# A fused decayed-attention, gated-MLP and max-MLP kernel: two chunks to one state rescale, row-wise gains, and a new order of steps

## The chip, the cores and the metric

The kernel runs on one core of a Trainium2 chip. The time is what the device reports for one execution of the whole program, in microseconds; a profiled execution has a span beside it, from the first to the last instruction. The engines named here are TensorE (PE: matrix products and transposes), VectorE (DVE), ScalarE (ACT), GpSimd (POOL) and SyncE (SP, which issues the transfers).

## The reference

Three stages follow each other. The first is a recurrence over 768 positions for 4 batches of 8 heads, with a state of 48 by 48 in a head; the decay of a position is complex and its magnitude is capped at 0.999.

```python
scale = np.minimum(mag, 0.999) / (mag + 1e-06)
a_re_n, a_im_n = (a_re * scale, a_im * scale)
for t in range(S):
    ar, ai = (a_re_n[:, :, t, :, None], a_im_n[:, :, t, :, None])
    new_re = ar * S_re - ai * S_im
    new_im = ar * S_im + ai * S_re
    kv = np.einsum('bhd,bhe->bhde', k[:, :, t], v[:, :, t])
    S_re, S_im = (new_re + kv, new_im)
    y[:, :, t] = np.einsum('bhd,bhde->bhe', q[:, :, t], S_re)
```

Its output, 3072 tokens of 384, goes through an MLP with a norm and a gate, and then through a product that keeps the largest of three.

```python
xn = x / rms * rms_g
silu = g * (1.0 / (1.0 + np.exp(-g)))          # g = xn @ w_gate
x = (silu * (xn @ w_val)) @ w_out              # 384 -> 1536 -> 384
h = np.maximum(np.maximum(x @ w1, x @ w2), x @ w3)
out = h @ w_out2                               # 384 -> 768 -> 384
```

The weights come as float64.

## The kernel before, in words

The positions are cut into six chunks of 128, and the batches into two pairs, which gives twelve units x0 to x11: unit n is the chunk n//2 of the pair n%2. A unit computes products of the decays inside a group of eight positions (the steps scan, VectorE), then across groups and up to the chunk's start (pre, many short steps on VectorE that write the tile G and the tile ET), spreads them (pa), multiplies them into q (qh) and their reciprocal into k (kr, kh), transposes both (tq, tk), and forms scores (qk), a mask (msk, GpSimd) and the output (pv). For the state that later chunks read it copies the scaled k into rows of positions by eight transfers on SP (kn1 and kn0, L801, tile kn), multiplies it with v on TensorE (kv0 and kv1, L912), and adds that to the state W (wa). As the decays are counted from the chunk's own start, the state is then rescaled by the decay of the whole chunk: a small product brings the decay into place (pw, L725, and t12, L730), two transfers swap the halves of W (wd, L929 and L930), and three steps on VectorE multiply and add (wu with x, y or z; they are recorded at the helper's line L341).

Two units give the 512 tokens of a block; blocks m0 to m5 run the MLP (g and v products at L1100 to L1102, then silu, gate, the split of the hidden values into two float16 parts uh and ul, and the products acc) and the max-MLP (h at the same lines, mx, hh, hl, and the output products om at L1254 to L1256). All weights and activations of the MLPs are float16 pairs, so each product is three. The blocks m0 and m1 are cut into two pieces of 256 tokens, each of which needs one unit alone. The steps big (L1243) keep a largest square for a range check at the end.

The float64 weights become float16 pairs in 60 conversions c0 to c59, each of 128 by 384: low (ScalarE, L421), join and sign (VectorE, L426 and L430), high (either of them), and for the lower half a difference, in 24 of the 60 as two products on TensorE (dif, L438 and L439) and otherwise on VectorE (rest). The first MLP's weights are multiplied by the gains rms_g, which gcl brings into the tile gsc (L382 and L383) and diag into the matrices down (L375). Transfers l0 to l59 read the weights once more, for a check of their range.

Every step has a name, and a table ORDER lists all the names in the order in which they are issued. Each engine takes its own instructions from that one list, strictly in order; a letter behind a name says which engine takes a step that could go to either. Semaphores, put in by the framework, make an instruction wait for its operands and for its buffer.

## Time and profile before

| what | value |
|---|---|
| three runs | 1017.63, 1018.71 and 1027.02 us; median 1018.71 us |
| profiled execution | 1017.69 us, its span 1016.0 us |
| TensorE busy | 941.9 us, 93% of the span |
| VectorE busy | 818.4 us, 81% |
| ScalarE busy | 462.5 us, 46% |
| GpSimd busy | 60.9 us, 6% |

A busy time is the union of the instructions' records and says nothing of who waits for whom. The page's strip of 40 slices shows where in the span an engine is busy, and at which share of full speed TensorE's clock was granted; the table by stretches gives the same for chosen stretches in microseconds; the timeline has the start, the duration and the idle time ahead of single instructions with what ended it.

### The profile page before, as it was taken

What the parts mean: (1) busy time and instruction counts of PE and PEld (TensorE: products, weight loads), DVE (VectorE), ACT (ScalarE), POOL (GpSimd) and SP (SyncE); (2) the same over time, 40 slices, a digit from 0 to 9 for tenths busy, and PEclk for the clock granted to TensorE, in tenths of its full rate; (3) what the DMA queues carried; (4) which work ended last, traced back from release to release, by engine and by line L of the source; (5) the groups of instructions that cost most, each with busy time, mean ns of one, the idle gap of its engine ahead of it and who ended that gap; (6) DMA issues with size and microseconds to landing.
All of it is one profiled execution on the core that took longest, in us unless ns stands there. A gap on an engine that the chain in (4) does not pass through costs nothing.

```text
span 1016.0 us, 16755 instructions
## 1 busy us (share of the span) xinstructions
PE 941.9 (93%) x6231; PEld 589.8 (58%) x6231; DVE 818.4 (81%) x1966; ACT 462.5 (46%) x877; POOL 60.9 (6%) x63
## 2 busy tenths in 40 slices
PE   1576998999999999999999999999999999999997
PEld 0254767855789886555556455556455565544443
DVE  4999999999899999649897488897459999875352
ACT  5666777665545573415563233643215352012110
POOL 1020010010010100000010001100000100000000
PEclk9677999999999999999999999999999999999999
DMA  6454565642231313023113023013012435872001
GB/s 170 125 144 133 129 174 147 187 130 57 66 74 44 65 53 69 16 54 67 34 47 76 1 59 86 9 47 75 1 44 70 118 109 174 260 235 62 1 1 35
DMA packets 84651, 87.50 MB, mean 86 GB/s; under 512 B 51920, under 2 KB 69200, under 8 KB 84560
## 3 DMA queue, kind: packets, MB, share of 16 engines
q1 hardware_dynamic: 84288, 85.95, 31.1%
q8 instruction: 51, 0.84, 0.3%
q10 hardware_dynamic: 272, 0.39, 0.2%
q14 instruction: 40, 0.33, 0.1%
HBM read 70.78 MB, written 4.72 MB: 74 GB/s over the span
## 4 chain that ended last, share of the span: by engine, by line
PE 71%; DVE 7%; ACT 1%; issue 1%; POOL 1%; DVEq 0%; ACTq 0%
PE gv L1100 7%; PE gv L1101 7%; PE gv L1102 7%; PE hm L1100 7%; PE hm L1101 7%; PE hm L1102 7%; PE yp L866 3%; PE acc L1100 3%; PE acc L1102 3%; PE acc L1101 3%; PE tp L810 3%; PE qk L834 3%; PE om L1254 2%; PE om L1256 2%; PE om L1255 2%; PE kp L912 2%
## 5 line engine op out<-in xcount | busy, mean ns | idle before, releaser
L849 POOL TENSOR_SCALAR_AFFINE_SELECT P<-P 128x512 f32<-128x512 f32 x48 | 57.4, 1205 | 780.1 <-ACT P L330 543.7
L1100 PE MATMUL gv<-XH,wvh 128*128 128x256 f16 (+1 forms) x288 | 94.4, 328 | 4.4 <-ACT sg L1128 4.4
L1102 PE MATMUL acc<-uh,wol 128*128 128x256 f16 (+1 forms) x288 | 93.9, 326 | 2.2 <-DVE wol L267 2.0
L1101 PE MATMUL gv<-XL,wgh 128*128 128x256 f16 (+1 forms) x288 | 94.3, 327 | 0.8 <-DVE XL L264 0.8
L1100 PE MATMUL gv<-XH,wgh 128*128 128x256 f16 (+1 forms) x288 | 94.3, 327 | 0.7 <-ACT XH L330 0.7
L1102 PE MATMUL gv<-XH,wvl 128*128 128x256 f16 (+1 forms) x288 | 94.4, 328 | 0.1
L1100 PE MATMUL acc<-uh,woh 128*128 128x256 f16 (+1 forms) x288 | 93.9, 326 | 0.6 <-ACT uh L330 0.2
L1101 PE MATMUL gv<-XL,wvh 128*128 128x256 f16 (+1 forms) x288 | 94.4, 328 | 0.0
L1102 PE MATMUL gv<-XH,wgl 128*128 128x256 f16 (+1 forms) x288 | 94.2, 327 | 0.0
L1101 PE MATMUL acc<-ul,woh 128*128 128x256 f16 (+1 forms) x288 | 93.8, 326 | 0.4 <-DVE ul L341 0.4
L267 DVE SCALAR_TENSOR_TENSOR sg<-gv,sg 128x256 f32<-128x256 f32 (+1 forms) x96 | 52.9, 552 | 49.9 <-PE gv L1102 49.6
L1128 ACT ACTIVATE sg<-gv 128x256 f32<-128x256 f32 (+1 forms) x96 | 46.5, 489 | 80.8 <-PE gv L1102 67.5
L267 DVE SCALAR_TENSOR_TENSOR hs<-hm,hs 128x512 f32<-128x512 f32 x72 | 49.5, 688 | 41.0 <-PE hm L1102 40.9
L341 DVE TENSOR_TENSOR ul<-sg,uh 128x256 f16<-128x256 f32 (+1 forms) x96 | 54.6, 571 | 6.7 <-ACT uh L330 6.3
L330 ACT CAST uh<-sg 128x256 f16<-128x256 f32 (+1 forms) x67 | 33.2, 498 | 54.5 <-DVE sg L267 48.5
L438 PE MATMUL dif<-cvc,down 128*128 128x384 f32 x48 | 27.2, 656 | 26.5 <-ACT down L375 20.2
L834 PEld LDWEIGHTS qk<-qT,kT 96*128 96x128 f32 x384 | 47.4, 194 | 5.1 <-issue 1.2
L834 PE MATMUL qk<-qT,kT 96*128 96x128 f32 x384 | 49.3, 279 | 0.9 <-ACT kT L330 0.7
L330 ACT CAST HH<-hs 128x512 f16<-128x512 f32 x25 | 15.4, 619 | 71.1 <-DVE hs L267 71.1
L352 ACT ACT_TABLE_LOAD x36 | 46.2, 1283 | 3.3 <-issue 2.7
L1254 PE MATMUL om<-uoh,HH 128*128 128x384 f16 x144 | 47.0, 326 | 0.0
L1256 PE MATMUL om<-uoh,HL 128*128 128x384 f16 x144 | 46.9, 326 | 0.0
(212 smaller groups left out, 2315.8 us busy)
## 6 DMA issues: line engine op xcount, KB each, us to landing
kn<-KH SPq DMA_DIRECT2D x160, 48.0 KB
raw<-in_moe_w_out_dram SPq DMA_DIRECT2D x18, 384.0 KB
raw<-in_moe_w_dram SPq DMA_DIRECT2D x18, 384.0 KB
lw<-in_moe_w_out_dram SPq DMA_DIRECT2D x18, 384.0 KB
lw<-in_moe_w_dram SPq DMA_DIRECT2D x18, 384.0 KB
ar<-in_a_re_dram SPq DMA_DIRECT2D x24, 192.0 KB
raw<-in_moe_w_gate_dram SPq DMA_DIRECT2D x12, 384.0 KB
raw<-in_moe_w_val_dram SPq DMA_DIRECT2D x12, 384.0 KB
```

What stands on the lines that cost most here:

```text
L267: nc.vector.scalar_tensor_tensor(out=o, in0=a, scalar=s, in1=b, op0=op0, op1=op1)
L330: nc.scalar.copy(o, i)
L341: eng[on(opts)].tensor_tensor(out=o, in0=a, in1=b, op=op)
L352: nc.scalar.preload_act_table_set(name)
L834: nc.tensor.matmul(p[:, j, :], lhsT=kT[:, h, :], rhs=qT[0:96, h, :], start=True, stop=True)
L849: nc.gpsimd.affine_select(out=P, in_=P, pattern=[[0, 4], [1, TP], [TP, TQ]], base=0, channel_multiplier=-1, compare_op=ALU.is_ge, fill=0.0)
L1100: nc.tensor.matmul(o, lhsT=wh, rhs=xh, start=first, stop=False)
L1101: nc.tensor.matmul(o, lhsT=wh, rhs=xl, start=False, stop=False)
L1102: nc.tensor.matmul(o, lhsT=wl, rhs=xh, start=False, stop=last)
L1128: nc.scalar.activation(s, L.pop(("g", j)), AF.Silu, scale=1.0 / (SW * SX))
L1254: nc.tensor.matmul(p, lhsT=hh[:, j, ts], rhs=WO2[0][:, j, :], start=(j == 0), stop=False)
L1256: nc.tensor.matmul(p, lhsT=hl[:, j, ts], rhs=WO2[0][:, j, :], start=False, stop=(j == NJ2 - 1))
```

## The change

Two tiles G take the place of one, one for each pair of batches. In the second chunk of two the products of the decays go on from the first chunk's (a step gs on GpSimd copies the first chunk's last product to the place where the second starts, and resets it after the second), so that the state needs its rescaling only after every second chunk: pw, t12, wd and wu are issued for the units x2, x3, x6 and x7 alone and no longer for ten units. The second chunk has one step more among the short ones (pre9, two instructions) and one fewer. The gains are loaded as three rows of 128 and transposed on TensorE (gtr). The first unit's decays, real and imaginary, are loaded from GpSimd's queue, where the real part came from SP's and the imaginary part from ScalarE's. The tile kn has one buffer instead of two. The steps big may go to ScalarE, and 14 of 18 do. The table ORDER is another one throughout.

```diff
@@ -49,7 +49,7 @@
                dwup=4.0, pw=66.0, ssq1=83.5, rstd=85.0)
 XSC = 1.0
 NW = 2 * KT * FF // CW + NJ + 3 * KT * FF2 // CW + NJ2
-KNB, YB, OBB = 2, 2, 2
+KNB, YB, OBB = 1, 2, 2
 WPOOL, LPOOL = 4, 1
 SPLIT = ()
 
@@ -286,7 +286,7 @@
     gsc = cst.tile([128, KT], F32, name="gsc")
 
     Tn = cst.tile([128, 4, 4, 32], F32, name="Tn")
-    G = cst.tile([128, 4, 5, 8], F32, name="G")
+    Gs = [cst.tile([128, 4, 5, 8], F32, name=f"G{z}") for z in range(2)]
 
     g_m2 = cst.tile([128, 2 * NP], F32, name="g_m2")
     g_n2 = cst.tile([128, 2, D], F32, name="g_n2")
@@ -375,16 +375,25 @@
             nc.scalar.mul(down[:, kt], ident, gsc[:, kt:kt + 1])
         nc.scalar.mul(less, ident, -1.0)
 
+    gains = []
+
     def ld_g():
-        nc.sync.dma_start(out=gts, in_=rms_g.rearrange("(k p) -> p k", p=128))
+        gains.append(xp.tile([KT, 128], F32, tag="m4", name="gr"))
+        nc.sync.dma_start(out=gains[0], in_=rms_g.rearrange("(k p) -> k p", p=128))
+
+    def gtr():
+        p = pat.tile([128, KT], F32, tag="p", name="gp")
+        nc.tensor.transpose(p, gains[0], ident[0:KT, 0:KT])
+        gains.append(p)
 
     def gcl():
-        nc.vector.tensor_scalar(out=gts, in0=gts, scalar1=5.9, scalar2=-5.9, op0=ALU.min, op1=ALU.max)
+        nc.vector.tensor_scalar(out=gts, in0=gains[1], scalar1=5.9, scalar2=-5.9, op0=ALU.min, op1=ALU.max)
         nc.vector.tensor_scalar(out=gsc, in0=gts, scalar1=-SW * 2.0 ** -128, scalar2=None, op0=ALU.mult)
 
     def one():
-        nc.gpsimd.memset(G, 0.0)
-        nc.gpsimd.memset(G[:, 0:4:3, 0, :], 1.0)
+        for G in Gs:
+            nc.gpsimd.memset(G, 0.0)
+            nc.gpsimd.memset(G[:, 0:4:3, 0, :], 1.0)
         nc.gpsimd.memset(g_n2, 1.0)
         nc.gpsimd.memset(g_ms, 1.0)
 
@@ -392,7 +401,7 @@
         for z in W + [qT]:
             nc.gpsimd.memset(z[96:128], 0.0)
 
-    for f in (con, tab, eye, sels, ld_g, gcl, diag, one, zero):
+    for f in (con, tab, eye, sels, ld_g, gtr, gcl, diag, one, zero):
         at("k", -20.0, f"k.{f.__name__}", f)
     jobs = []
 
@@ -517,6 +526,10 @@
 
         b0, i = where(n)
         last = i == NCH - 1
+
+        second = i % 2 == 1
+        carry = second and not last
+        G = Gs[n % 2]
         L = {}
         T = T_CHAIN
         PS = parts(n)
@@ -529,7 +542,7 @@
                 b0, i = where(n)
                 t = xp.tile([128, 2, TP, D], F32, tag=nm, name=nm)
                 for jb in range(2):
-                    dma = nc.scalar if n == 0 and nm == "ai" else nc.sync
+                    dma = nc.gpsimd if n == 0 and nm[0] == "a" else nc.sync
                     dma.dma_start(out=t[:, jb].rearrange("p t d -> p (t d)"),
                                   in_=src[b0 + jb, :, C * i:C * i + C, :].rearrange("h (q t) d -> h q (t d)", q=TQ))
                 ops[n, nm] = t
@@ -662,17 +675,18 @@
                 if k < 3:
 
                     m, x, y, o = L["m4"][r, 0], T[:, k, 0:2], T[:, k + 1], T[:, k + 1]
-                elif k < 6:
-                    g = k - 2
+                elif k < 6 or k == 9:
+                    g = k - 2 if k < 6 else 0
                     m = L["m4"][r, 0, :, :, 0:8]
-                    x, y, o = Gr[:, 0:2, g] if g > 1 else T[:, 3, 0:2, 0:8], T[:, 3, :, 8 * g:8 * g + 8], Gr[:, :, g + 1]
+                    x = Gr[:, 0:2, g] if g > 1 or second else T[:, 3, 0:2, 0:8]
+                    y, o = T[:, 3, :, 8 * g:8 * g + 8], Gr[:, :, g + 1]
                 else:
                     j = k - 6
                     m, x = L["m4"][r, 0], T[:, j, 0:2]
                     y = Gr[:, :, 0:4]
                     o = z and L["ET"][r].rearrange("p c (h g j) -> p j c g h", g=4, j=4)[:, j + 1]
                 if z == 0:
-                    if k >= 6:
+                    if 6 <= k < 9:
                         x = x.rearrange("p c (g h) -> p c g h", g=4)
                         for w in range(2):
                             tt(m[:, w].rearrange("p c (g h) -> p c g h", g=4), y[:, 2 * w:2 * w + 2],
@@ -680,16 +694,28 @@
                     else:
                         tt(m, x[:, :, None, :].to_broadcast(m.shape), y.rearrange("p (w c) h -> p w c h", w=2), ALU.mult)
                 elif z == 1:
-                    i = [m[:, w].rearrange("p c (g h) -> p c g h", g=4) if k >= 6 else m[:, w] for w in range(2)]
-                    tt(o if k >= 6 else o[:, 0:2], i[0], i[1], ALU.add)
+                    i = [m[:, w].rearrange("p c (g h) -> p c g h", g=4) if 6 <= k < 9 else m[:, w] for w in range(2)]
+                    tt(o if 6 <= k < 9 else o[:, 0:2], i[0], i[1], ALU.add)
                 elif k == 2:
                     four(o, m, b)
                 elif k == 3:
                     nc.vector.tensor_copy(Gr[:, :, 1], T[:, 3, :, 0:8])
                 else:
-                    nc.vector.tensor_scalar(out=Gr[:, 2, 2:4], in0=Gr[:, 1, 2:4], scalar1=-1.0, scalar2=None, op0=ALU.mult)
-                    nc.vector.tensor_copy(Gr[:, 3, 2:4], Gr[:, 0, 2:4])
-            return f
+                    g = slice(1 if second else 2, 4)
+                    nc.vector.tensor_scalar(out=Gr[:, 2, g], in0=Gr[:, 1, g], scalar1=-1.0, scalar2=None, op0=ALU.mult)
+                    nc.vector.tensor_copy(Gr[:, 3, g], Gr[:, 0, g])
+            return f
+
+        def gs():
+
+            if second:
+                nc.gpsimd.memset(G[:, 1:3, 0, :], 0.0)
+                nc.gpsimd.memset(G[:, 0:4:3, 0, :], 1.0)
+            else:
+                nc.gpsimd.tensor_copy(G[:, 0:2, 0], G[:, 0:2, 4])
+                nc.gpsimd.tensor_scalar(out=G[:, 2, 0], in0=G[:, 1, 4], scalar1=-1.0, scalar2=0.0, op0=ALU.mult,
+                                        op1=ALU.add)
+                nc.gpsimd.tensor_copy(G[:, 3, 0], G[:, 0, 4])
 
         def et(b):
             def f():
@@ -1017,11 +1043,14 @@
             e("pt", f"pt{x}", pt(b))
             e("pt", f"ptc{x}", ptc(b))
             for lv in range(9):
-                for z in range(2):
+                if lv == 3 and second:
+                    for z in range(2):
+                        e("pre", "pre9" + "xy"[z] + x, pre(9, z, b), T["dpre"] * lv)
+                for z in range(0 if lv == 5 and last else 2):
                     e("pre", f"pre{lv}" + "xy"[z] + x, pre(lv, z, b), T["dpre"] * lv + (0.1 if lv > 5 else 0.0))
                 if lv == 2:
                     e("pre", f"pre{lv}z{x}", pre(lv, 2, b), T["dpre"] * lv)
-                if lv in (3, 4):
+                if lv == 4 or lv == 3 and not second:
                     e("pre", f"pre{lv}z{x}", pre(lv, 2, b), T["dpre"] * lv)
                 if lv == 5:
                     e("pre", f"et{x}", et(b), T["dpre"] * lv)
@@ -1060,12 +1089,15 @@
             if not last:
                 e(f"kv{jb}", f"kv{jb}", kv(jb))
                 e(f"kv{jb}", f"wa{jb}", wa(jb))
+            if carry:
                 e(f"kv{jb}", f"wd{jb}", wd(jb))
                 for z in range(3):
                     e(f"kv{jb}", f"wu{jb}" + "xyz"[z], wu(jb, z), T["dwup"])
-        if not last:
+        if carry:
             e("pw", "pw", pw)
             e("pw", "t12", t12)
+        if not last:
+            e("pw", "gs", gs)
         for b, x in PS:
             for z in range(2 + 3 * len(NEWT)):
                 e("rstd", f"rs{z}{x}", rstd(z, b))
@@ -1240,9 +1272,12 @@
             def f():
                 xh, _ = X1[blk]
                 s = mw.tile([128, N], F32, tag="sg", name="junk1", bufs=SGB)
-                nc.vector.tensor_tensor_reduce(out=s, in0=xh[:, o], in1=xh[:, o], scale=1.0, scalar=0.0,
-                                               op0=ALU.mult, op1=ALU.max,
-                                               accum_out=g_x1[:, KT * blk + o:KT * blk + o + 1])
+                top = g_x1[:, KT * blk + o:KT * blk + o + 1]
+                if on("av") == "a":
+                    nc.scalar.activation(s, xh[:, o], AF.Square, accum_out=top)
+                else:
+                    nc.vector.tensor_tensor_reduce(out=s, in0=xh[:, o], in1=xh[:, o], scale=1.0, scalar=0.0,
+                                                   op0=ALU.mult, op1=ALU.max, accum_out=top)
             return f
 
         def om(t):
...
@@ -1374,274 +1409,270 @@
 
 
 ORDER = """
-k.con x0.ld_ai k.eye x0.ld_ar k.tab k.one k.zero k.sels c0.load c14.load c10.load x0.ld_v0 k.ld_g x0.sq1/v x0.ld_k
-x0.ld_v1 x0.ld_q x0.sq0/a x0.m20 x0.m21 c0.low x0.ln c0.join c0.sign c4.load c14.low x0.nt0 c14.join c14.sign c10.low
-x0.nt1 c9.load k.gcl x0.nu c0.high/a c14.high/a x0.nt2/a k.diag x0.ai c0.dif x0.aim c10.join c14.dif x0.ain/a x1.ld_ai
...
+k.con k.eye c1.load k.tab c5.load x0.ld_ar k.ld_g k.sels c0.load x0.ld_k x0.ld_ai x0.ld_q x0.ld_v0 c1.low x0.ld_v1
+c1.join k.zero c1.sign c5.low c4.load c5.join c5.sign x0.sq0/a k.one k.gtr c3.load k.gcl k.diag c5.high/a c5.dif
+c0.low c1.high/v c0.join c1.dif c5.rest/v c0.sign c0.high/v c12.load c0.dif c1.rest/a x0.sq1/a c0.rest/a x0.m21 x0.m20
+x0.ln x0.nt0 x0.nt1 x0.nu c4.low x0.nt2/v c4.join x0.ai c3.low c4.sign c3.join c10.load c4.high/a c4.dif x0.ar c12.low
+c3.sign x0.aim c9.load c3.high/a c3.dif c4.rest/a c12.join x1.ld_ai x0.ain/a c12.sign x0.ar0/a c3.rest/a x0.scan1y
+c14.load x0.scan1x c10.low x0.scan1z c12.high/a c12.dif c10.join x0.scan2x x0.scan2y c12.rest/a c10.sign c9.low
...
```

What the new table does to the engines is shown at three places. The first is the start of the program on SP, the queue of the transfers (ar, ai, q, k and v are the first unit's inputs, raw is a weight's words, gts and gr the gains). Before:

```order
L533 DMA ar<-in_a_re_dram 128x1x384 x2
L402 DMA raw<-in_moe_w_gate_dram 128x768
L402 DMA raw<-in_moe_w_val_dram 128x768
L402 DMA raw<-in_moe_w_gate_dram 128x768
L542 DMA v<-in_v_dram 128x8x48
L379 DMA gts<-in_moe_rms_g_dram 128x3x1
L533 DMA k<-in_k_dram 128x1x384 x2
L542 DMA v<-in_v_dram 128x8x48
L533 DMA q<-in_q_dram 128x1x384 x2
```

Now:

```order
L411 DMA raw<-in_moe_w_gate_dram 128x768
L411 DMA raw<-in_moe_w_val_dram 128x768
L382 DMA gr<-in_moe_rms_g_dram 3x128
L411 DMA raw<-in_moe_w_gate_dram 128x768
L546 DMA k<-in_k_dram 128x1x384 x2
L546 DMA q<-in_q_dram 128x1x384 x2
L555 DMA v<-in_v_dram 128x8x48 x2
L411 DMA raw<-in_moe_w_val_dram 128x768 x3
```

The weights' words now come first, the gains third, and the decays have left this queue; on GpSimd's they stand behind the making of the identity matrix.

The second place is VectorE's first instructions (Rn and Zn hold the squares and magnitudes of the decays, cvc a weight on its way, gts and gsc the gains). Before:

```order
L357 MEMSET consts 128x1
L358 MEMSET consts 128x1
L348 TENSOR_TENSOR Rn<-ai 128x768
L558 ISA Zn,g_m_88<-Zn,Rn 128x384
L558 ISA g_m_88 128x1
L558 ISA Zn,g_m_88<-Zn,Rn 128x384
L558 ISA g_m_88 128x1
L426 SCALAR_TENSOR_TENSOR cvc<-raw 128x384
L430 SCALAR_TENSOR_TENSOR cvc<-raw,cvc 128x384
L426 SCALAR_TENSOR_TENSOR cvc<-raw 128x384
L430 SCALAR_TENSOR_TENSOR cvc<-raw,cvc 128x384
```

Now:

```order
L435 SCALAR_TENSOR_TENSOR cvc<-raw 128x384
L439 SCALAR_TENSOR_TENSOR cvc<-raw,cvc 128x384
L435 SCALAR_TENSOR_TENSOR cvc<-raw 128x384
L439 SCALAR_TENSOR_TENSOR cvc<-raw,cvc 128x384
L390 TENSOR_SCALAR gts<-gp 128x3
L391 TENSOR_SCALAR gsc<-gts 128x3
L338 TENSOR_SCALAR wgh<-cvc,gsc 128x384
L435 SCALAR_TENSOR_TENSOR cvc<-raw 128x384
L336 CAST wvl<-dif 128x384
L439 SCALAR_TENSOR_TENSOR cvc<-raw,cvc 128x384
L338 TENSOR_SCALAR wgh<-cvc,gsc 128x384
L571 ISA Zn,g_m_89<-Zn,Rn 128x384
```

Two conversions, the gains and parts of a third conversion now stand ahead of the first sum of squares (the ISA row on Zn), one of whose squares has left for ScalarE.

The third place is SP's queue where the first unit's k rows are copied (kn). Before:

```order
L533 DMA k<-in_k_dram 128x1x384 x2
L801 DMA kn<-KH 128x1x96 x8
L402 DMA raw<-in_moe_w_val_dram 128x768
L402 DMA raw<-in_moe_w_out_dram 128x768
L801 DMA kn<-KH 128x1x96 x8
L402 DMA raw<-in_moe_w_out_dram 128x768
L533 DMA ai<-in_a_im_dram 128x1x384 x2
```

Now:

```order
L546 DMA k<-in_k_dram 128x1x384 x2
L827 DMA kn<-KH 128x1x96 x8
L411 DMA raw<-in_moe_w_val_dram 128x768 x2
L546 DMA ai<-in_a_im_dram 128x1x384 x2
L411 DMA raw<-in_moe_w_val_dram 128x768
L411 DMA raw<-in_moe_w_gate_dram 128x768
L411 DMA raw<-in_moe_w_out_dram 128x768
L555 DMA v<-in_v_dram 128x8x48
L827 DMA kn<-KH 128x1x96 x8
```

Before, the two sets of eight transfers stand two weights apart and go to two buffers. Now they have one buffer, and eight other transfers stand between them; the second set waits until the first one's product (kv0 on TensorE) has read it.

## Rows read from the trace of the kernel before

**Rows 1.** The page: busy times, then the busy tenths and the granted clock in 40 slices.

```profile
PE 941.9 (93%) x6231; PEld 589.8 (58%) x6231; DVE 818.4 (81%) x1966; ACT 462.5 (46%) x877; POOL 60.9 (6%) x63
...
PE   1576998999999999999999999999999999999997
...
DVE  4999999999899999649897488897459999875352
...
PEclk9677999999999999999999999999999999999999
```

**Rows 2.** Table by stretches: stretch, its length, busy us of each engine, clock, DMA.

```profile
0.00:85.65 85.65, 41.56 (x207) 26.29 (x208) 69.10 (x188) 52.05 (x107) 9.23 (x19) 0.78 0.56 154
85.65:255.20 169.55, 154.13 (x1179) 112.96 (x1179) 164.65 (x411) 116.62 (x245) 9.68 (x8) 0.98 0.48 131
255.20:425.80 170.60, 167.57 (x1436) 131.44 (x1435) 156.13 (x399) 90.86 (x178) 12.85 (x12) 1.00 0.24 58
425.80:1016.00 590.20, 578.59 (x3412) 319.12 (x3410) 428.56 (x970) 202.96 (x349) 29.13 (x24) 1.00 0.26 72
...
320.50:378.30 57.80, 55.11 (x535) 49.01 (x534) 54.55 (x145) 37.32 (x74) 3.97 (x4) 1.00 0.25 62
```

**Rows 3.** Timeline: first products of blocks m0 and m1; start, duration, engine, idle before.

```profile
85.65 0.27 PE L1100 MATMUL gv<-XH,wgh 128*128 128x256 f16 x1 [0.72 <-ACT XH L330]
...
255.21 0.27 PE L1100 MATMUL gv<-XH,wgh 128*128 128x256 f16 x1
```

**Rows 4.** Timeline of the first 24 us: the gains' transfer and the first waits.

```profile
4.88 2.56 SPq L379 DMA_DIRECT2D gts<-in_moe_rms_g_dram  x1
...
8.94 0.84 ACT L346 ACTIVATE Zn<-ar 128x768 f32<-128x768 f32 x1 [4.40 <-DMA ar<-in_a_re_dram]
...
11.00 0.96 DVE L348 TENSOR_TENSOR Rn<-ai 128x768 f32<-128x768 f32 x1 [10.01 <-DMA ai<-in_a_im_dram]
...
17.75 0.17 DVE L383 TENSOR_SCALAR gsc<-gts 128x3 f32<-128x3 f32 x1
...
20.15 1.65 PE L438 MATMUL dif<-cvc,down 128*128 128x384 f32 x2 [20.15 <-ACT down L375]
```

**Rows 5.** VectorE's groups by form: count, busy us, mean ns of one, idle before.

```profile
L430 DVE SCALAR_TENSOR_TENSOR cvc<-raw,cvc 128x384 int32<-128x384 int32 x60 | 33.4, 562 | 0.3
L426 DVE SCALAR_TENSOR_TENSOR cvc<-raw 128x384 int32<-128x384 int32 x60 | 33.2, 555 | 3.7 <-ACT raw L421 3.6
...
L558 DVE CUSTOM_DVE_ANT_0 Zn<-Zn,Rn 128x384 f32<-128x384 f32 x24 | 14.3, 603 | 0.5 <-ACT Zn L346 0.4
L1243 DVE CUSTOM_DVE_ANT_0 junk<-X1H 128x512 f32<-128x512 f16 x18 | 13.5, 751 | 0.1
...
L264 DVE TENSOR_TENSOR m<-G,Tn 128x64 f32<-128x64 f32 x72 | 13.0, 222 | 1.3
...
L341 DVE TENSOR_TENSOR W<-W,T 96x384 f32<-96x384 f32 x20 | 10.9, 547 | 0.4 <-DMA Ws<-W 0.4
...
L336 DVE COPY P<-qk 128x512 f32<-128x512 f32 x14 | 9.5, 685 | 0.3 <-PE qk L834 0.2
```

**Rows 6.** TensorE's groups: the conversions' and the rescaling's products.

```profile
L438 PE MATMUL dif<-cvc,down 128*128 128x384 f32 x48 | 27.2, 656 | 26.5 <-ACT down L375 20.2 <-DVE cvc L430 6.3
L725 PE MATMUL pw<-G,sel 128*96 128x8 f32 x80 | 8.1, 227 | 0.0
```

**Rows 7.** Timeline: the copies of k, and a transfer that VectorE waited for.

```profile
57.05 5.15 SPq L801 DMA_DIRECT2D kn<-KH  x8
...
699.15 1.06 SPq L930 DMA_DIRECT2D Ws<-W  x1
...
701.85 0.73 DVE L341 TENSOR_TENSOR Ws<-Ws,T 96x384 f32<-96x384 f32 x1 [0.34 <-DMA Ws<-W]
```

**Rows 8.** Waits, longest first: total us, times, the longest.

```profile
PE gv L1100 <- ACT sg L1128: 4.4, 1, 4.4
...
SPq L402 <- DVE cvc L430: 79.8, 43, 5.0
```

More of the change, by code (lines that the diff above doesn't have):

```diff
@@ new lines @@
+x1.sq1/a x0.scan4x x0.scan4z c9.high/a c9.dif x0.scan5y x0.scan5x x0.scan5z c14.low x0.scan6x c9.rest/a x0.scan6y
+c14.join x0.scan6z c14.sign c11.low x0.scan7x c6.load c14.high/a c14.dif x0.scan7y x1.ld_ar c11.join x0.scan7z
+c14.rest/a c11.sign x0.pt c2.low c11.high/v c7.load c11.dif x0.ptc c2.join c2.sign c11.rest/a x0.pre0x c21.load
+c2.high/a c2.dif x0.pre0y x0.pre1x c6.low x0.pre1y x0.pre2x c2.rest/a c6.join x0.pre2y x0.pre2z c6.sign x0.pre3x
+x0.pre3z c8.load c6.high/a x0.pre3y x0.pre4x x0.pre4y c6.rest x1.sq0/a x0.pre5x x0.pre4z x0.pre5y x0.pre6x x0.et
```

518 lines of the change are left out of this document (253 added, 265 removed).

## The prediction

> **What bounds the kernel now.** I first read the busy times and the strip of 40 slices [rows 1]: TensorE is busy for 93% of the span, yet its strip starts at 1 and reaches a steady 9 only after a quarter, while VectorE's stands at 8 and 9 from the second slice to the fourteenth. An average therefore hides two regimes, and I cut the span at products that exist in both kernels: the first g product of block m0 at 85.65 us and that of m1 at 255.21 us [rows 3]. The table by stretches [rows 2] then says what bounds each.
>
> - Start, to 85.65 us: TensorE works 41.56 us, part of it at half clock (0.78 on average), VectorE 69.10. The end of this stretch is a chain through unit x0, most of it on VectorE, which does nothing until 11.00 us because it waits for the imaginary decays [rows 4].
> - Middle, 85.65 to 255.20: VectorE is busy 164.65 of 169.55 us, TensorE 154.13. VectorE bounds it; the 15.4 us that TensorE idles are waits for it, directly or through ScalarE (the longest is 4.4 us, for a silu on ScalarE [rows 8]).
> - Late, from 255.20: TensorE is busy 167.57 of 170.60 us and then 578.59 of 590.20. It bounds both stretches; what VectorE saves there is worth nothing, and only TensorE's own work counts.
>
> So a saving on VectorE pays in the middle alone, one on TensorE late, and what moves ahead of m0's first product costs at the start.
>
> **The change, stretch by stretch.** I counted the steps of both tables between the same products and priced the differences with durations of the profile.
>
> *Start.* Ahead of m0's first product stand 6 more joins and 5 more signs of conversions: 6 x 0.555 + 5 x 0.562 = 6.1 us on VectorE [rows 5]. Other moves: two squares go to ScalarE, 2 x 0.96 less [rows 4]; two more high parts, a score's copy (0.685 [rows 5]) and a step of the norm come to VectorE, two copies leave it; together +1.2. Net +5.4 us. Five more differences are done on TensorE here, which waits in this stretch anyway. Ahead of the first scan the chain is also another one: the gains' transfer takes 2.56 us to issue and gsc is written at 17.75 us, so that TensorE's first product comes at 20.15 us [rows 4]; now three rows of gains bring this forward, and VectorE meets the copy of a difference before its first sum of squares. That copy waits for ScalarE (square of ar, down) and for a product that took 1.65 us at half clock, so part of the 10 us of early idleness fills and a new wait takes its place. I let the two cancel and take +5.4, because everything behind x0's last scan is in VectorE's order, and from there to m0 I count the same 55 us in both tables. Bounds: +1 if the two conversions at the head (4 x 0.56 = 2.2 us) and the third one's start fit into the idle 10 us; +9 if the decays land later from GpSimd's queue. This trace has no transfer from that queue. Nearest are ar and ai themselves, ready 8.94 and 11.00 us after the span's start: the same bytes behind 0.8 MB of weights may be some 4 us later, or earlier, since SP's issue no longer stands before them.
>
> The Trainium skill, SBUF — State Buffer, section "SBUF: two separate sides", speaks against the new queue: GpSimd writes its transfers' descriptors itself and is locked out while VectorE runs certain instructions with two ports. If each of the four conversion instructions at the head held it up, the decays would come 2.2 us later and the sum would be 2.2 us higher, still inside the bound of +9. No run so far shows such a transfer.
>
> *Middle.* On VectorE: 6 joins and 5 signs fewer, -6.1; 12 rescaling instructions fewer (5 state updates of 3 become 1), 12 x 0.547 = -6.6; the three steps big of m0 leave for ScalarE, 3 x 0.751 and the reads of their sums, -2.5; one unit's two magnitude sums fall behind m1's first product, 2 x 0.603 = -1.2; 14 short steps of the decays likewise, some at 0.222 and the rest shorter, -3; placements of single steps (more high parts, mx and uh, fewer copies) +3.5 [rows 5]. Net -16, so 164.65 becomes 148.6 us. On TensorE five differences leave (27.2 us for 24 of them in their first half alone, at mixed clocks [rows 6]; 0.9 each at full clock) and one rescaling product (8 records at 0.227, of which several overlap, 0.6): 154.13 - 5.1 = 149.0. The two engines now need the same, so neither one's sum is the length. The nearest row of such a balance is 320.50 to 378.30 [rows 2]: VectorE 54.55, TensorE 55.11, length 57.80, that is 1.049 of the busier engine. 149.0 x 1.049 = 156.3, or -13.2 against 169.55. Bounds: 149.0 without a gap (-20.5), and 162 (-7.5) if VectorE keeps the 4.9 idle microseconds it has now and TensorE's waits through ScalarE come on top.
>
> *Late.* Four rescaling products fewer (seven before, three now), -2.5; of VectorE's remaining 24 rescaling instructions, the nine steps big that go to ScalarE there and all other placements I count nothing, as TensorE's queue covers them: VectorE is busy 428.56 of 590.20 us. If that cover went, some 20 us of VectorE's savings would count too. The output products of each block now stand ahead of the next block's first product and not behind it; both lie in the late stretches, so their sum is unchanged. The tail after the last product has the same steps. Bounds: -4 to +3.
>
> *The single buffer of kn.* The second set of copies now starts when the first set's product is done. It takes 5.15 us to issue, and a transfer inside the chip was waited for until 1.6 us after its issue (699.15 + 1.06 to 701.85) [rows 7], so 6.9 us go by until the second product may run; whatever stands behind it on TensorE, MLP products among it, waits too. TensorE's own work between the two products, from the order: 4.5 us for x0 (where VectorE has 8 and sets the pace), 7.7 for x3, 7.9 for x8, 10.9 for x6, 12.2 for x5, 15.5 for x4, over 19 for the others. All but x0 are over 6.9: I cost it at nothing, with the slack of x3 and x8, under 1 us, as the place to look.
>
> GpSimd's small copies (gs) stand between masks and are needed a unit later: nothing.
>
> **Sum.** 1016.0 + 5.4 - 13.2 - 2.5 = 1005.7 us of span. The profiled execution lies 1.7 us above its span (1017.69), so 1007.4 us. That profiled execution is itself 1.0 us under the median of the three runs, 1018.71; against the median the forecast is -1.1%. One per cent, 10.2 us, is about what a measurement of this kernel can tell from no change: the bounds of "within" are 1008.5 and 1028.9.
>
> **The rivals.**
>
> *More than forecast.* The head's conversions fit into the early wait (+1 instead of +5.4) and the middle runs without gaps (149.0 instead of 156.3): 1007.4 - 4.4 - 7.3 = 995.7. For it: the strip shows VectorE's first slice at 4. Against it: the balanced stretch of the trace lost 5%. Chance 0.17.
>
> *The freed time turns into idle time.* TensorE keeps its waits in the middle, because the chain of a unit runs through ScalarE, masks and transfers and not through VectorE's sum; only its own 5.1 us or less go. Start +5.4, middle -5 to 0, late -2.5: 1015.6 to 1020.6, about 1018. For it: the 4.4 us wait on ScalarE [rows 8]. Against it: VectorE at 97% of that stretch. Chance 0.18.
>
> *The decays come late.* Held up on GpSimd's queue, they shift unit x0 by 2.2 to 4 us more than I took, 1009.6 to 1011.4. Nothing in this trace speaks for or against it. Chance 0.06.
>
> *Slower: kn's single buffer becomes the bound.* SP issues in order, and a transfer of weights ahead of the second set may hold it; such holds reach 5.0 us now [rows 8]. With a hold of h, TensorE stands still for 6.9 + h less its work between the products, in each unit where that is positive: with h = 7, 9.4 (x0) + 6.2 (x3) + 6.0 (x8) + 3.0 (x6) + 1.7 (x5) = 26 us, or 1033.7. It decides from h = 6, where the sum passes 21.5 us. Against it: the order leaves at most three weight transfers ahead of the set, and none in x3 to x9. Chance 0.10. Other mishaps of that sign: 0.02.
>
> That the rescaling is really gone from six units is plain in the order (24 instructions on W remain of 60).
>
> **How the numbers follow.** My forecast has the remaining 0.47, with some 6 us to either side; as it lies 1.1 us below the bound, 0.28 of that is faster and 0.19 within. Faster: 0.28 + 0.17 = 0.45. Within: 0.19 + 0.18 + 0.06 = 0.43. Slower: 0.12. The range for 8 in 10 reaches from the first rival to the upper end of the second, 996 to 1021, and leaves out the slower one.
>
> **What would show it.** In the profile of the changed kernel: m0's first product at 91 us (right within 87 to 95) and m1's at 247; between them VectorE busy about 149 us and TensorE's wait for silu gone; TensorE without a gap from m1 on, apart from at most 1 us ahead of the second kn product of x3 and x8. Wrong would be: m0's first product later than 95 us with VectorE waiting for a decay (start), TensorE idle over 10 us in the middle (second rival), or TensorE waiting on kn in several units (slower).

## The result, and the profile after

The changed kernel takes 1009.16 us (median of 4 runs, 1007.93 to 1009.98) against 1018.78 us for the kernel before (4 runs, 1017.63 to 1027.02) on the same chip: ratio 0.9893, 95% interval 0.9846 to 0.9940. Timed again beside experiments, with five runs, it gave 0.9892 (0.9875 to 0.9909). So it is faster by about 1% (the medians of the first four runs alone give 0.9906, and one of the four runs before, 1027.02 us, lies 8 us above the others). The forecast was 1007.4 us, or -1.1% against the median.

Its profiled execution took 1007.93 us with a span of 1006.2 us, 9.8 us under the span before. Three parts make that difference. The page, busy times and strips of 40 slices, in answer to [rows 1]:

```profile
PE 938.2 (93%) x6184; PEld 588.9 (59%) x6184; DVE 792.3 (79%) x1912; ACT 464.0 (46%) x887; POOL 62.6 (6%) x95
...
PE   2548997999999999999999999999999999999996
...
DVE  4899999999977989847889655989734999978451
...
PEclk8758998999999999999999999999999999999999
```

The average says little again: TensorE is busy 3.7 us less, VectorE 26 us less. Where that counted, the table by stretches tells, cut at the same products as [rows 2]. Its columns are the stretch, its length, then the busy times of TensorE, its weight loads, VectorE, ScalarE and GpSimd, the clock and the DMA load:

```profile
0.00:94.45 94.45, 46.78 (x216) 28.16 (x217) 73.93 (x198) 59.16 (x122) 11.05 (x28) 0.76 0.59 160
94.45:251.12 156.67, 148.47 (x1156) 112.15 (x1156) 151.10 (x374) 106.09 (x223) 11.17 (x13) 0.96 0.45 125
251.12:431.90 180.78, 179.73 (x1516) 139.90 (x1515) 157.43 (x427) 93.70 (x177) 16.61 (x20) 1.00 0.23 56
431.90:1006.20 574.30, 563.20 (x3300) 308.72 (x3298) 409.88 (x916) 205.05 (x367) 23.72 (x34) 1.00 0.26 71
```

| stretch | before | after | difference | forecast |
|---|---|---|---|---|
| start, to m0's first product | 85.65 | 94.45 | +8.8 | +5.4 |
| middle, to m1's first product | 169.55 | 156.67 | -12.9 | -13.2 |
| late, to the end | 760.8 | 755.1 | -5.7 | -2.5 |

The cut inside the late stretch at 425.80 us before and 431.90 us after moves, because the output products of m1 now stand ahead of it; only the sum of the two is to be compared. TensorE's part of that sum fell from 746.2 to 742.9 us.

In the middle TensorE idles 8.2 us, most of it at one place: a product pw waits 3.43 us for a step on VectorE, and two shorter waits of 1.39 and 0.87 us follow within 5 us. Behind the first of them the granted clock is at half for 6.8 us. VectorE is busy for 6.96 us of the 7.00 shown, so the half clock need not have cost time there:

```profile
157.63 0.82 PE L751 MATMUL pw<-G,sel 128*96 128x8 f32 x8 [3.43 <-DVE rz L264]
...
158.50:165.50 7.00, 4.77 (x21) 3.24 (x22) 6.96 (x20) 4.76 (x13) 0.15 (x2) 0.52 0.45 115
```

In the start, the timeline shows the new head (start, duration, engine, idle before and what ended it), in answer to [rows 4]:

```profile
7.63 0.17 DVE L391 TENSOR_SCALAR gsc<-gts 128x3 f32<-128x3 f32 x1
...
9.62 0.84 ACT L346 ACTIVATE Zn<-ar 128x768 f32<-128x768 f32 x1 [3.27 <-DMA ar<-in_a_re_dram]
10.37 0.97 ACT L375 ACTIVATE down<-ident,gsc 128x128 f32<-128x128 f32 x3
...
11.39 1.65 PE L447 MATMUL dif<-cvc,down 128*128 128x384 f32 x2 [6.01 <-ACT down L375]
...
13.13 0.56 DVE L435 SCALAR_TENSOR_TENSOR cvc<-raw 128x384 int32<-128x384 int32 x1 [4.87 <-PE dif L447]
...
16.24 0.56 DVE L571 CUSTOM_DVE_ANT_0 Zn<-Zn,Rn 128x384 f32<-128x384 f32 x1 [1.17 <-ACT Rn L346]
...
20.19 0.96 DVE L341 TENSOR_TENSOR AA<-Zn,AA 128x768 f32<-128x768 f32 x1 [2.90 <-ACT AA L590]
```

The gains are there at 7.63 us and not at 17.75. But the matrices down, which are ready to go from then on, stand on ScalarE behind the square of ar, and that waits until 9.62 us. So the first difference starts at 11.39 us, VectorE waits 4.87 us for it, and its first sum of squares comes at 16.24 us, where it came at 12.11. The step nt1, the row at 20.19 us, came at 16.68 us before:

```profile
12.11 0.56 DVE L558 CUSTOM_DVE_ANT_0 Zn<-Zn,Rn 128x384 f32<-128x384 f32 x1
...
16.68 0.95 DVE L341 TENSOR_TENSOR AA<-Zn,AA 128x768 f32<-128x768 f32 x1
17.55 0.16 DVE L382 TENSOR_SCALAR gts<-gts 128x3 f32<-128x3 f32 x1
```

The last of these rows, from the kernel before, corrects the forecast's reading of 17.75 us. VectorE had no idle time ahead of the step that reads the gains, so it did not wait for their transfer: its own order put the step there.

The groups of instructions that the change touches, in answer to [rows 5, 6] (count, busy us, mean ns of one, idle before):

```profile
L1277 ACT ACTIVATE junk<-X1H 128x512 f32<-128x512 f16 x14 | 8.8, 628 | 11.4 <-DVE HL L341 11.4
L341 DVE TENSOR_TENSOR W<-W,T 96x384 f32<-96x384 f32 x8 | 4.4, 547 | 0.0
L751 PE MATMUL pw<-G,sel 128*96 128x8 f32 x32 | 3.1, 223 | 3.4 <-DVE rz L264 3.4
L1279 DVE CUSTOM_DVE_ANT_0 junk<-X1H 128x512 f32<-128x512 f16 x4 | 2.7, 684 | 0.1
```

Of the 20 multiplications of W by the decay 8 are left, of 80 records of pw 32, and 14 of the 18 steps big are on ScalarE.

In the late stretch TensorE's waits, longest first, answer to [rows 8]. The long one for a silu is gone, none names kn, and none is over 1.2 us; in all TensorE stands 4.2 us between m1's first product and its last. It is SP's queue that waits for kn's single buffer (the last row, for the whole span: four times, 16.5 us in all, 8.8 us at most), which the kernel before never does:

```profile
PE pf L1364 <- DVE lo L1362: 1.2, 1, 1.2
PE pt L647 <- DVE AA L264: 1.1, 1, 1.1
PE pn L1358 <- DVE top L264: 0.8, 1, 0.8
...
SPq L827 <- PE kp L938: 16.5, 4, 8.8
```

### The profile page after: what moved, and what is told of

The parts are those of the page before. It is cut to its first block, busy times and chain, and to the rows that moved or that the text cites. A ratio compares the mean times of both kernels' runs of the same rounds, so it can differ in the third digit from the quotient of the medians.

```text
span 1006.2 us, 16626 instructions
## 1 busy us (share of the span) xinstructions
PE 938.2 (93%) x6184; PEld 588.9 (59%) x6184; DVE 792.3 (79%) x1912; ACT 464.0 (46%) x887; POOL 62.6 (6%) x95
## 4 chain that ended last, share of the span: by engine, by line
PE 68%; DVE 9%; issue 1%; ACT 1%; DMA 0%; DVEq 0%; ACTq 0%
PE gv L1132 7%; PE gv L1134 7%; PE gv L1133 7%; PE hm L1132 6%; PE hm L1133 6%; PE hm L1134 6%; PE acc L1133 3%; PE acc L1132 3%; PE acc L1134 3%; PE yp L892 3%; PE qk L860 3%; PE tp L836 3%; PE om L1289 2%; PE om L1291 2%; PE om L1290 2%; PE kp L938 2%
## 5 line engine op out<-in xcount | busy, mean ns | idle before, releaser
L875 POOL TENSOR_SCALAR_AFFINE_SELECT P<-P 128x512 f32<-128x512 f32 x48 | 49.8, 1046 | 596.4 <-ACT P L330 409.0
L330 ACT CAST uh<-sg 128x512 f16<-128x512 f32 (+1 forms) x69 | 35.2, 511 | 77.6 <-DVE sg L267 61.2
L341 DVE TENSOR_TENSOR ul<-sg,uh 128x256 f16<-128x256 f32 (+1 forms) x96 | 53.9, 566 | 12.9 <-ACT uh L330 12.4
L1290 PE MATMUL om<-uol,HH 128*128 128x384 f16 x144 | 46.9, 326 | 0.0
L435 DVE SCALAR_TENSOR_TENSOR cvc<-raw 128x384 int32<-128x384 int32 x60 | 35.6, 593 | 12.0 <-ACT raw L430 6.2
```

Source lines behind the costliest of these rows:

```text
L341: eng[on(opts)].tensor_tensor(out=o, in0=a, in1=b, op=op)
L435: nc.vector.scalar_tensor_tensor(out=L["c"], in0=raw[:, :, 1], scalar=3, in1=raw[:, :, 0], op0=ALU.logical_shift_left, op1=ALU.bitwise_or)
L875: nc.gpsimd.affine_select(out=P, in_=P, pattern=[[0, 4], [1, TP], [TP, TQ]], base=0, channel_multiplier=-1, compare_op=ALU.is_ge, fill=0.0)
L1290: nc.tensor.matmul(p, lhsT=hh[:, j, ts], rhs=WO2[1][:, j, :], start=False, stop=False)
```

## The experiments

Ratios are to the kernel before, run on the same chip in the same group, with 95% intervals. The changed kernel stands at 0.9892 in them. Where a text says how many microseconds lie between an experiment and the changed kernel, it is the difference of these ratios, since the groups ran on two chips; 1 us is 0.001.

**1. The two-chunk rescaling alone, in the old order.** The kernel before with

```diff
+        second = i % 2 == 1
+        carry = second and not last
...
+            if carry:
                 e(f"kv{jb}", f"wd{jb}", wd(jb))
```

and the steps gs and pre9; nothing else of the change. So that two tiles G and both buffers of kn fit, a scratch tile is kept in bfloat16 and a tile of the range check lies in another buffer.

> The kernel before with the two-chunk rescaling alone: its own order, queues, gains and both buffers of kn. Theory (the rescaling's own instructions count where VectorE bounds, its products where TensorE does): the stretch from m0's to m1's first product loses 12 VectorE instructions of 0.547 us, some 6 us, the late stretch four products of pw, some 2.5 us, the start nothing: about 1010 us, ratio 0.992. Rival (the new order brings the gain): within 2 us of 1018.8.

Measured: 1017.93 us, 0.9989 (0.9974 to 1.0004). The rival's number came. Yet the instructions are gone: the middle stretch of this kernel against [rows 2], and below it the first 4 us of it, where the columns are as before:

```profile
85.80:256.10 170.30, 156.19 (x1171) 113.64 (x1171) 160.58 (x400) 116.53 (x244) 10.99 (x13) 0.97 0.46 128
...
85.80:90.00 4.20, 3.52 (x16) 2.27 (x16) 4.06 (x16) 1.89 (x3) 1.14 (x3) 0.50 0.34 98
```

The same 4 us in the kernel before:

```profile
85.65:90.00 4.35, 3.48 (x29) 2.85 (x29) 4.28 (x17) 1.69 (x3) 0.00 (x0) 1.00 0.32 90
```

VectorE is busy 4.1 us less, and the stretch is 0.8 us longer: VectorE's idle time in it grew from 4.9 to 9.7 us. TensorE ran m0's first products at half clock here (0.50, 16 of them) where it ran them at full clock before (1.00, 29), the product pb behind them came 2.0 us later (91.56 and 89.53 us), and VectorE waited 1.8 us for what follows from it. How much of that the other runs have is not known: this execution, at 1019.38 us, is the slowest of eleven. The late stretch lost nothing either (761.6 and 760.8 us): TensorE is busy 2.1 us less in it (744.0), close to the theory's 2.5, and idle 2.9 us more. In the old order the freed time became idle time.

**2. Rescaling after every chunk again, in the new order.** The changed kernel with

```diff
-        second = i % 2 == 1
-        carry = second and not last
+        second = False
+        carry = not last
```

and the steps wd, wu, pw and t12 of six units put back into the table; gs and pre9, which the longer products need, go out. First with wu 12 steps behind wd and t12 right behind pw:

> The changed kernel with the state rescaled after every chunk again, all else (order, gains, queues, single kn buffer, big on ScalarE) as changed. Theory: the stretch from m0's to m1's first product gains 12 VectorE instructions, some 6.6 us, the late stretch some 2.5 us of products: about 1018 us. Rival (the new order hides the rescaling's work): 1009 to 1012 us.

Measured: 1050.97 us, 1.0307 (1.0286 to 1.0327). Neither number came. VectorE's waits name a part of what my spacing did:

```profile
DVE Ws L341 <- DMA Ws<-W: 26.0, 7, 5.0
```

Then with more room:

> The changed kernel with the state rescaled after every chunk again, now with 30 steps of the order between the swap of W's halves and the three VectorE steps that need it, and 6 between pw and t12. Theory (the 42 us of the first trial were waits for swaps placed too close, VectorE's 26 us on Ws the longest; the work itself is 18 x 0.547 us on VectorE, of which a third lies in the stretch that VectorE bounds, and six products of 0.6 us): 8 to 12 us above the changed kernel, ratio 0.998 to 1.002. Rival (SP's queue, where the swaps stand among transfers of words, is what costs): 20 us or more.

Measured: 1028.77 us, 1.0084 (1.0059 to 1.0109), nearly 20 us above the changed kernel. The theory's 8 to 12 us are missed. The rival's 20 us came, but not its reason: VectorE's waits for Ws are down to 6.0 us in all, and nothing else shows SP's queue as the cause. The stretches read:

```profile
0.00:98.90 98.90, 49.30 (x224) 29.49 (x225) 75.81 (x202) 59.53 (x123) 9.86 (x25) 0.73 0.58 158
98.90:260.60 161.70, 149.99 (x1164) 113.33 (x1164) 155.05 (x381) 106.03 (x224) 9.73 (x8) 0.95 0.44 122
```

The middle has 5.0 us more than in the changed kernel. Nine of the twelve instructions on W stand in it here, 9 x 0.547 = 4.9 us, so there the term holds. The other three stand in the start, which has 4 to 5 us more, 1.8 of them a wait for Ws. The late stretch has 13 more (768.1 against 755.1), of which 7.3 are TensorE's busy time. The places are mine and not tuned, so 20 us is what this placing costs, an upper bound for the work. With experiment 1: taking the rescaling out of the order made for it brought nothing that these runs can tell from none, and putting it into the other cost time.

**3. All steps big on VectorE.** The table with /v behind all 18:

```diff
-m0.big0/a ... m1.big1/a ... m5.big2/a
+m0.big0/v ... m1.big1/v ... m5.big2/v
```

> The changed kernel with all 18 steps big on VectorE. Theory: the three of block m0 stand in the stretch that VectorE bounds, 3 x 0.751 and the reads of their sums, +2.5 us, the others lie behind TensorE: about 1011.7 us. Rival (VectorE does not bound the stretch any more, TensorE does): 1009 us, no difference.

Measured: 1014.71 us, 0.9957 (0.9942 to 0.9972), 6.6 us above the changed kernel. More than the theory's 2.5. The profiled execution, 1016.09 us, is the slowest of six. The stretches of this kernel, with five microseconds behind the range check's last product:

```profile
95.20:253.40 158.20, 149.63 (x1157) 112.76 (x1157) 152.56 (x379) 103.83 (x217) 10.96 (x13) 0.95 0.44 123
253.40:1014.40 761.00, 746.19 (x4814) 448.57 (x4812) 574.09 (x1364) 291.31 (x522) 40.08 (x54) 1.00 0.25 67
979.69:984.69 5.00, 5.00 (x16) 1.99 (x17) 1.71 (x4) 0.51 (x1) 0.00 (x0) 0.66 0.02 5
```

and of the changed kernel, run again in the next group:

```profile
94.21:250.60 156.39, 149.11 (x1156) 112.67 (x1156) 150.60 (x373) 106.36 (x223) 12.73 (x13) 0.95 0.45 124
250.60:1005.70 755.10, 743.08 (x4814) 448.66 (x4812) 566.93 (x1342) 298.70 (x544) 40.31 (x54) 1.00 0.25 68
972.78:977.78 5.00, 5.00 (x24) 2.34 (x25) 2.40 (x5) 1.22 (x2) 0.00 (x0) 1.00 0.02 5
```

The middle pays 1.8 us. The late stretch, where I had counted these moves at nothing, pays 5.9 us and is as long as in the kernel before (760.8). Of that, 3.1 us are TensorE's busy time and 2.8 idle time in pieces: the wait ahead of the range check's first product is 1.3 us instead of 0.8, and several of 0.1 to 0.9 us are new. About 1.7 us of the busy time came from one place: behind TensorE's waits at the range check the granted clock fell, and 16 products ran in 5 us instead of 24. That part need not belong to the steps big, as it also comes in experiment 4, where 14 of them are on ScalarE. Without it they are worth some 4.2 us here.

Experiments 4, 5 and 8 share their group with the changed kernel itself:

> The changed kernel as it is, timed beside the others of this group: 1008 to 1010 us, ratio 0.990 to the kernel before, by every theory; it is the base for the other three.

Measured: 1006.77 us, 0.9892 (0.9875 to 0.9909).

**4. Two buffers of kn again.** KNB = 2, with the scratch tile in bfloat16 and the range check's tile in another buffer for room.

> The changed kernel with two buffers for kn again; the room comes from a scratch tile of the norm kept in bfloat16 (its values are not read). Theory (the order gives each second set of copies time enough, so the single buffer costs nothing): within 1 us of the changed kernel. Rival (the second sets hold SP's queue and with it transfers of words that VectorE waits for): 2 to 4 us faster.

Measured: 1009.71 us, 0.9918 (0.9903 to 0.9934). Not faster: its median is 2.9 us above the changed kernel's in the same group, at the edge of the intervals and outside the theory's 1 us. In its profile, the slowest execution of six, 1.7 us stand at the range check again, where the clock fell to 0.66 over 5 us behind waits of 0.8 and 1.2 us.

**5. The gains element by element.**

```diff
-        nc.sync.dma_start(out=gains[0], in_=rms_g.rearrange("(k p) -> k p", p=128))
+        nc.sync.dma_start(out=gts, in_=rms_g.rearrange("(k p) -> p k", p=128))
```

> The changed kernel with rms_g loaded element by element as before, without the transpose. Theory (VectorE takes its steps in order, and the gains stand fifth): gsc is written at about 17.7 us and not at 7.6, the first sum of squares comes some 8 to 10 us later, and so does m0's first product: about 1018 us. Rival (the start hangs on the decays' landing, and the gains land in their shadow): 1009 to 1011 us.

Measured: 1008.46 us, 0.9910 (0.9894 to 0.9926). My theory fell. The gains' step on VectorE and the square of ar:

```profile
7.12 0.27 DVE L384 TENSOR_SCALAR gts<-gts 128x3 f32<-128x3 f32 x1
...
10.83 0.84 ACT L346 ACTIVATE Zn<-ar 128x768 f32<-128x768 f32 x1 [4.84 <-DMA ar<-in_a_re_dram]
```

Issued third, single elements are there when VectorE comes to them, as rows are. In the kernel before, VectorE's order put the step at 17.55 us, so that time says nothing of how late they landed. What the rows may bring is that ar comes about 0.4 to 1.2 us earlier (10.39 and 9.62 us in two profiles); the time does not tell the two apart.

**6. The old queues for the first decays.**

```diff
-                    dma = nc.gpsimd if n == 0 and nm[0] == "a" else nc.sync
+                    dma = nc.scalar if n == 0 and nm == "ai" else nc.sync
```

> The changed kernel with the first decays on their old queues: the real part on SP's behind two weights, the imaginary part on ScalarE's. Theory (the queue that issues hardly matters, the transfers share the same 16 engines): ar is ready within 1 us of 9.6 us, and the time is within 2 us of the changed kernel. Rival (GpSimd's queue is the slower one): 2 to 4 us faster.

Measured: 1010.46 us, 0.9912 (0.9888 to 0.9936): 2 us above, not told apart from none. When ar was ready the profile does not show, as ScalarE came to it only at 10.99 us. The profile shows how the queue can matter, though not by what I had in mind:

```profile
8.19 1.86 ACTq L546 DMA_DIRECT2D ai<-in_a_im_dram  x2
10.11 0.98 ACT L430 ACTIVATE raw<-raw 128x384 int32<-128x384 uint32 x2 [7.46 <-DMA ai<-in_a_im_dram]
...
23.04 0.96 DVE L341 TENSOR_TENSOR AA<-Zn,AA 128x768 f32<-128x768 f32 x1 [2.90 <-ACT AA L590]
```

ScalarE does nothing for 7.46 us at the issue of ai before it does the low parts of the first two conversions. The issue itself takes 1.86 us of that. It starts only at 8.19 us, because in the trace it waits for a semaphore that it shares with the second transfer of ar: the wait is for ar to land. So the step nt1 comes at 23.04 us (20.19 and 20.97 in the changed kernel) and m0's first product at 97.3. On GpSimd such a wait would hold up only small memsets, and in the changed kernel's profile there is none: both transfers are issued by 4.05 us.

**7. Another order for the start.** On ScalarE the squares go behind the matrices down, on VectorE the sums of squares ahead of the third conversion:

```diff
-c5.sign x0.sq0/a k.one k.gtr c3.load k.gcl k.diag c5.high/a c5.dif c0.low c1.high/v c0.join c1.dif c5.rest/v
+c5.sign k.one k.gtr c3.load k.gcl k.diag c1.high/v c5.high/a c5.dif c1.dif x0.sq0/a c0.low x0.sq1/a x0.m21 x0.m20
```

> The changed kernel with the first 30 steps in another order: the two squares of the first unit's decays behind the diagonal matrices on ScalarE, and its sums of squares and logarithm ahead of the third conversion's join. Theory (VectorE's early idle time of 4.9, 1.2 and 2.9 us is a wait for the first difference, behind a square that waits for ar): the step nt1 comes 4 us earlier, and m0's first product with it: about 1005 us. Rival (the time comes back at the next conversions, whose words land late, or VectorE's sum sets the start): 1008 to 1009 us.

Measured: 1005.85 us, 0.9872 (0.9851 to 0.9893), and in the profile

```profile
12.43 0.84 ACT L346 ACTIVATE Rn<-ai 128x768 f32<-128x768 f32 x1 [1.35 <-DMA ai<-in_a_im_dram]
...
17.25 0.96 DVE L341 TENSOR_TENSOR AA<-Zn,AA 128x768 f32<-128x768 f32 x1 [1.04 <-ACT AA L590]
...
90.68 0.37 PE L1132 MATMUL gv<-XH,wgh 128*128 128x256 f16 x1 [0.57 <-ACT XH L330]
```

nt1 comes 3 to 4 us earlier and m0's first product 3.5 to 3.8, and at the end 2.0 to 2.5 are left (1003.7 of span against 1005.7 and 1006.2). The intervals of the two ratios overlap, so that the gain in time is likely, not certain; the gain at the start is plain in the profile. The early wait was one of order, not of data.

**8. The decays ahead of everything.**

```diff
-k.con k.eye c1.load k.tab c5.load x0.ld_ar k.ld_g k.sels c0.load x0.ld_k x0.ld_ai x0.ld_q x0.ld_v0 c1.low x0.ld_v1
+k.con x0.ld_ar x0.ld_ai k.eye k.tab k.ld_g c1.load c5.load k.sels c0.load x0.sq0/a x0.sq1/a c1.low x0.m21 x0.m20
```

> The reordered start with the decays ahead of all weights: the real part first on SP's queue, the imaginary part first on GpSimd's, q, k and v later, the squares first on ScalarE, sums and logarithm ahead of the conversions. Theory (the decays wait for their share of the transfers behind 0.8 MB of weights, k and q): ai is ready at about 7 us and not at 12.4, nt1 at about 12 and not at 17.3, and VectorE is idle some 3 us less in all, as conversions move behind: m0's first product at 87 to 88 us, about 1003 us. Rival (the transfers are not the limit, or the conversions' words then come late): 1005 to 1008 us.

Measured: 1006.84 us, 0.9902 (0.9883 to 0.9921), no better than the changed kernel. The rival. The decays come early as expected, and then the words are late:

```profile
8.95 0.82 ACT L346 ACTIVATE Rn<-ai 128x768 f32<-128x768 f32 x1
...
9.80 0.56 DVE L571 CUSTOM_DVE_ANT_0 Zn<-Zn,Rn 128x384 f32<-128x384 f32 x1 [8.82 <-ACT Rn L346]
...
13.75 0.96 DVE L341 TENSOR_TENSOR AA<-Zn,AA 128x768 f32<-128x768 f32 x1 [1.11 <-ACT AA L590]
...
22.80 0.56 DVE L435 SCALAR_TENSOR_TENSOR cvc<-raw 128x384 int32<-128x384 int32 x1 [2.09 <-ACT raw L430]
```

Up to nt1 VectorE idles 10.9 us, about as long as in experiment 7 (11.4), now in one piece at the head; behind nt1 it idles 9.0 us instead of 4.6, and m0's first product is back at 94.0 us.

**9. The reordered start, and the range check in five steps.** The step ok is cut at its two products, and these go between h products:

```diff
-m5.mx30/v m5.big2/a ok m5.h32 m5.mx31 m5.h40 m5.mx32
+m5.mx30/v m5.big2/a ok m5.h32 okp m5.mx31 okr m5.h40 okt m5.mx32 okf
```

> The start reordered as in the run before last group, and the range check at the end in five steps instead of one, its two small products on TensorE one and two h products later than the steps of VectorE that feed them. Theory (TensorE waits 0.8 and 1.2 us for VectorE there, and at times its clock falls to half behind them, which cost a further 1.5 us in one profile): 2 us or more below the reordered start alone, ratio 0.985 to the kernel before. Rival (the waits come back as VectorE's later steps hold the h products): 0.987.

Measured: 1003.77 us, 0.9848 (0.9829 to 0.9866), a further 2.4 us below experiment 7, as the theory said, though the two intervals overlap. The late stretch bears it out: with the check in one step it took 754.7 to 756.0 us in six profiles (the changed kernel twice, experiments 5 to 8; in experiment 4, with its fallen clock, 759.7), now 752.0 us here and 751.7 us in experiment 10. TensorE goes through the check without a stop:

```profile
967.42 0.33 PE L1363 MATMUL pn<-top,ones 128*128 128x60 f32 x2
...
969.53 0.27 PE L1374 MATMUL pf<-ident,lo 128*1 128x128 f32 x1
...
246.70:998.70 752.00, 742.40 (x4814) 448.56 (x4812) 566.95 (x1342) 298.60 (x544) 40.31 (x54) 1.00 0.25 68
```

**10. The split check with a third start.**

> As the run with the split check, with another start: the first weight, then the decays (real part on GpSimd's queue, imaginary part on SP's), then all other weights, q, k and v later; diagonal matrices ahead of the squares, the second conversion in the shadow of the logarithm. Theory (VectorE is idle 8 us instead of 11 until nt1): m0's first product at 88 us instead of 90.7, ratio 0.982. Rival (what is gained at the head is lost at the third to fifth conversion, whose words land later, as with the decays ahead of everything): 0.985 to 0.988.

Measured: 1002.44 us, 0.9832 (0.9816 to 0.9849). In its profile m0's first product stands at 93.4 us, not at 88, so the gain I meant did not come: nt1 is at 15.19 us, but VectorE idles 11.1 us until then, not 8, and the next words are late. The ratio came near the theory's 0.982 all the same, without its reason. Its time is not told apart from the one before. Both versions beat the changed kernel by 4 to 6 us, and the kernel before by 1.5 to 1.7%.

## Why the prediction was right, and where it was not

The sum came out 0.5 us under the measured span (1005.7 and 1006.2), but two terms were mis-sized, the start by 3.4 us and the late stretch by 3.2, and balance each other. That the sum is so close is luck; that the middle carries the gain is not.

*The middle, -13.2 forecast, -12.9 measured.* VectorE was to need 148.6 us and TensorE 149.0; they needed 151.1 and 148.5. The factor from the balanced stretch, 1.049, made 156.3 of it; 156.67 came. Here too two errors met: the factor on the measured 151.1 would have given 158.5, and the stretch was only 1.037 of it. What its parts are worth singly is another matter: the rescaling is 5.0 us by experiment 2 (for nine of the twelve instructions) and nothing by experiment 1, the steps big 1.8 by experiment 3 (2.5 forecast). The conversions that moved out of this stretch, 6.1 us, are argued from the order and were not tried alone, so that the middle's gain is shown in parts only.

*The start, +5.4 forecast, +8.8 measured, just inside the bound.* VectorE's work grew by 4.8 us (69.10 to 73.93; 5.8 in the changed kernel's second profile), close to the 5.4. The step that failed is "I let the two cancel": idle time did not stay the same but grew by 4.0 us (2.8 in the second profile). Before nt1 it is 14.2 us instead of 12.5 (15.0 in the second); behind the step pt it is 5.7 instead of 2.6 (3.8 in the second), there with waits of 1.4 us for a copy from ScalarE and 0.6 us for a difference, which the second does not have. I had seen that VectorE's copy would wait for "ScalarE (square of ar, down)", and took the trade as even without adding up the times: ar at 8.94 us, plus 0.84 for the square, 0.97 for the matrices and 1.65 for the product, is past 12 us, when the kernel before was already at its sums. (That this product ran at half clock, as the forecast has it, is a guess from its length: the granted clock reads 1.00 there.) Experiment 7 shows that this wait came from order alone. The decays themselves were hardly late: GpSimd issued both by 4.05 us, and ar was ready at 9.62 us, 0.7 us later than before (10.39 us in the second profile), and nothing waited for ai.

The section of the Trainium skill on the two sides of SBUF (SBUF — State Buffer, "SBUF: two separate sides") had spoken against that queue. Here it decides nothing: GpSimd had issued both transfers before VectorE began its first conversion at 4.92 us, so no run here shows the lock-out of a descriptor that it tells of.

*The late stretch, -2.5 forecast, -5.7 measured, beyond the bound of -4.* The sign was right, its reason covers at most a small part. The four products of pw were all I counted, and experiment 1, which drops them with the rest of the rescaling, makes this stretch no shorter. The steps big I counted at nothing, "as TensorE's queue covers them" (nine of them by my count, eleven in fact); experiment 3 puts them back on VectorE and gets the late stretch of the kernel before, 761.0 us. So most of this gain is the steps big: some 4.2 us, without the clock's part in that profile. Whether the rest, 1.5 us, is pw's products stays open. VectorE is busy for 75% of that stretch, which I read as cover. It is cover on the average. Where TensorE waits for VectorE's next small result, a step big ahead of it in VectorE's queue can count; that this is how the 4.2 us come about is argued from the new short waits of experiment 3. "TensorE without a gap from m1 on" did not come either: it stands 4.2 us in pieces of up to 1.2.

*The single buffer of kn, nothing forecast, nothing measured.* No wait of TensorE for kn stands in the profile, and a second buffer does not help. SP's queue was held as the rival has it, four times and once for 8.8 us; with two buffers these holds are gone, and the kernel is no faster, so they cost nothing. (Of the rival's own sum: a hold of 6 us gives 21.3, just under the 21.5 it was to pass.) The rival that ended slower is out, and so is the late landing of the decays. Of "the freed time turns into idle time" experiment 1 is the pure case: alone, the rescaling's saving did just that, as VectorE's idle time in the middle grew from 4.9 to 9.7 us. With the new order VectorE idles 5.6 us there.

## What to carry to other kernels

Price an instruction at the place where it stands: the same rescaling was worth nothing to take out of an order built around it, and cost up to 20 us put into one that was not. When a change moves work on one engine, write down for the first waits of the chain when each operand is there in either version, rather than cancelling waits against each other. A short wait of a fully loaded TensorE can cost more than its length, as its clock may fall behind it: two waits of 0.8 and 1.2 us at a check are gone when one step is split, and the late stretch is 2.7 to 4.3 us shorter.
